# Head 0's queries in two halves, scores of one half beside the maxima of the other

## The chip, the cores and the metric

One NeuronCore of one Trainium2 chip runs the whole program. The metric is device time in microseconds (us), the median of several executions. Engines: TensorE multiplies (PE, its weight load PEld), VectorE (DVE), ScalarE (ACT) and GpSimd (POOL) compute, SyncE (SP) issues most DMAs.

## The reference, cut to what matters

Hashed-bucket attention (16 heads of 768 x 64), then two feed-forward layers over 1536 tokens. The change touches the attention alone.

```python
q_bits = (einsum(q, proj) > 0); k_bits = (einsum(k, proj) > 0)      # 6 bits
mask   = bucket(q_bits)[:, None] == bucket(k_bits)[None, :]
scores = where(mask, q @ k.T / sqrt(64), -1e9)
attn   = exp(scores - scores.max(-1)); attn = attn / (attn.sum(-1) + 1e-9)
x      = attn @ v                       # then x -> two feed-forward layers
```

## The kernel before, in words

Everything is float32; operands of TensorE are split into a rounded high part and a low part (`qB` and `qX` for queries, `KK[:, 0]` and `KK[:, 1]` for keys). Rows 0 to 13 of `qB` and `KK` hold the codes of the buckets as +-1 and large numbers, so that one product gives score and mask together; one more row carries minus the maximum of each query. A query's row maximum is taken from rounded operands first (`smax`, L392: two matmuls of 384 columns, then one reduction on VectorE over 2 x 385 PSUM columns, the last of each bank a fixed bound). The row of maxima goes into `qB`. Then `st` (L437) computes the transposed scores of 128 keys by 768 queries with four matmuls, and ScalarE takes Exp straight from PSUM into the tile `E[c]`. `pair` adds two such tiles on GpSimd, `pv` multiplies by the values, `dsum` sums the denominators.

Work is issued in slots, six for a head; slot 6h + c has `st(h, c)`, `smax(h + 1, c)` and whatever else is due. Each engine runs its own instructions in the order in which the program writes them. Before slot 0 comes a list written by hand, `start`, with its helpers: `get` and `load` (DMAs), `khi`, `qhi`, `klo`, `qlo` (head 0's splits), `codes` (code products), `code_k` on VectorE and `code_q` on ScalarE (signs into `KK` and `qB`), `warm(n)` (n products of ones, each shown as two entries, that do nothing but keep TensorE busy), `ident` (identity for the transpose), `row0` (head 0's maxima, turned from a column into a row by six matmuls with the identity; for the other heads `fin_a` on VectorE and the DMA `fin_b` do that), `move_k`, `move_x`, `move_h` (copies from one group of partitions to another by DMA). `hi` and `lo` split the heads behind. PSUM is eight banks, as four tiles `T` of two, given out in turn by `two_banks`.

Head 0 in `start`: its loads, products for codes, signs, six `smax`, head 1's codes, `row0`, then slot 0 begins with all 768 queries' scores.

Of the kernel before, what the change touches and what calls it, by code (L numbers as in the profile page):

```python
# [27 lines left out]
NBITS = 6  # L28
QUAD = S // 4
OLD = 3  # L30
EARLY = 7
W_AT, W_LEAD = 11, 6
POOL_LO = (("lo", 1), ("lo", 2))
# [14 lines left out]
def attention_moe_moe(ctx: ExitStack, tc: tile.TileContext, kq, v, proj2, cst, eye, w1, w2, ab, out):  # L48
# [11 lines left out]
    def f32(ap):  # L60
        return ap.bitcast(F32)
# [7 lines left out]
    def lo_pool(o, i, h):  # L69
        nc.gpsimd.tensor_tensor(out=o, in0=i, in1=f32(h), op=ALU.subtract)  # L70
# [88 lines left out]
    def attention(actx, tctx):  # L159
# [10 lines left out]
        ring[0] = pool(actx, "ring0", RING[0])  # L170
        ps = pool(actx, "ps", 1, space=PSUM)
        T = [ps.tile([128, 2, 512], F32, tag=f"s{i}", name=f"s{i}") for i in range(4)]
        turn = [0]
        ahead = []

        def two_banks():
            if ahead:
                return ahead.pop()
            turn[0] += 1
            return T[(turn[0] - 1) % 4]  # L180

# [19 lines left out]
        def memsets():  # L201
            nc.vector.memset(ones, 1.0)
            nc.vector.memset(wones, 1.0)
            for t in E:
                nc.gpsimd.memset(t[:, :, HALF:HALF + 2], GUARD / S)
            for t in T:
                nc.vector.memset(t[:, :, HALF:HALF + 1], -BIG / 4)
            nc.gpsimd.memset(f32(qB[0])[0:64], 0.0)
            pad(0, nc.gpsimd)
            pad(1, nc.vector)  # L210
            for i in range(2):
                nc.gpsimd.memset(f32(SM[i]), 0.0)
# [19 lines left out]
        def load(h):  # L232
            if not 0 <= h < B * H:
                return
            b, hh = divmod(h, H)
            if h == 0:
                home[0] = wpool.tile([128, 2, 2 * DM], F32, tag=f"w{EARLY - 1}", name="kq")
            raws[h] = home[0][:, h % 2, 0:S]
            nc.sync.dma_start(out=raws[h], in_=kq[b, hh])


        def load_v(j):
            if 0 <= j < B * H // 2:
# [13 lines left out]
                fn(qX[h % NB], raws[h], qB[h % NB])  # L257


        def khi(i):  # L260
            o = KK[0][64:128, i] if i < 2 else qX[0][0:64]
            nc.scalar.activation(out=o, in_=raws[0][0:64], func=ACT.Copy)

        def qhi():
            nc.vector.tensor_copy(qB[0][64:128], raws[0][64:128])

        def qlo():
            lo_pool(qX[0][64:128], raws[0][64:128], qB[0][64:128])

        def klo():  # L270
            lo_pool(qX[0][0:64], raws[0][0:64], qX[0][0:64])

        def move_k(h):
            if 0 <= h < B * H:
# [39 lines left out]
        def codes(h):  # L314
            if not 0 <= h < OLD:
                return
            p = [two_banks() for _ in range(1 + (h == 0))]
            ct[h] = p[0][:, 0], p[-1][:, 1]
            code_products(h)


        def warm(n):
            if not ahead:
                ahead.append(two_banks())
            for _ in range(n):
                nc.tensor.matmul(out=ahead[0][0:32, 0, 0:128], lhsT=ones, rhs=wones, start=True, stop=True)

        def code_k(h, of=(0, 1)):
            if not 0 <= h < OLD:
# [54 lines left out]
                )  # L384


        def signs(h):
            for a in range(2):
                code_k(h, (a,))
                code_q(h, (1 - a,))  # L390

        def smax(h, c):  # L392
            if not 0 <= h < B * H:
                return
            p = two_banks()
            m = SM[h % 2][:, c:c + 1] if h else Z[:, 32 + c:33 + c]
            for a in range(2):
                nc.tensor.matmul(  # L398
                    out=p[:, a, 0:HALF], lhsT=qB[h % NB][:, c * 128:(c + 1) * 128], rhs=qhalf(KK[h % NB][:, 0], a),
                    start=True, stop=True,  # L400
                )
            nc.vector.tensor_reduce(out=m, in_=p[:, :, 0:HALF + 1], op=ALU.max, axis=AX.XY)  # L402


        def fin_a(h):
# [10 lines left out]
                out=f32(qB[h % NB])[ROW:ROW + 1].rearrange("o (c i) -> o c i", c=NC), in_=ST[h % 2][0:NC],  # L416
            )

        def row0():
            p = two_banks()  # L420
            for c in range(NC):
                nc.tensor.matmul(
                    out=p[0:64, c // 3, c % 3 * 128:c % 3 * 128 + 128], lhsT=Z[:, c:c + 64], rhs=I_t,
                    start=True, stop=True,
                )
            nc.vector.tensor_copy(qhalf(qB[0], 1)[32:33], p[32:33, 1, 0:HALF])
            nc.scalar.activation(out=qhalf(qB[0], 0)[32:33], in_=p[32:33, 0, 0:HALF], func=ACT.Copy)

        def ident():
            hi_pool(I_t, I_f)  # L430
# [3 lines left out]

        pt = {}

        def st(h, c):  # L437
            if not 0 <= h < B * H:
# [12 lines left out]
            nc.scalar.activation(out=E[c][:, :, 0:HALF], in_=halves(p), func=ACT.Exp, scale=1.0 / D ** 0.5)  # L451
# [205 lines left out]
        def get(i):  # L657
# [2 lines left out]
            )[i]  # L660
            (nc.sync if i else nc.scalar).dma_start(out=t, in_=d)

        def coef():
# [12 lines left out]
        def run():  # L676
            memsets()
            fns = {o[0]: o[1] for o in order}
            fns.update(get=get, coef=coef, khi=khi, qhi=qhi, qlo=qlo, klo=klo, signs=signs, row0=row0, ident=ident, spare=spare)
            done.update((name, (0,)) for name in ("hi", "lo", "move_k", "code_ka", "code_kb", "code_q", "fin_b"))  # L680
            for name, *k in start:
                if name == "warm":
                    warm(*k)
# [237 lines left out]
        return run  # L921

    with tc.manual_schedule():
        nc.scalar.preload_act_table_set("natural_log_exp_and_others")
        tctx = ExitStack()
        with ExitStack() as actx:
            run, tail = attention(actx, tctx)
# [59 lines left out]
```

## Time and profile before

| what | value |
|---|---|
| median of 3 runs | 734.08 us (734.04 to 735.63) |
| the profiled execution | 734.39 us, of which its span 732.6 us |
| TensorE busy | 724.3 us, 99% of the span |
| VectorE, ScalarE, GpSimd busy | 575.9, 416.4, 130.3 us |
| DMA | 82.89 MB, mean 113 GB/s |

Times of rows count from the span's start. In a row, the name before the arrow is what is written, the one behind it what is read. `x8` is a count of merged instructions; a bracket gives the engine's idle time before the group and what ended it. Matmul ends are modelled, so a busy TensorE is not one at its peak; a float32 product of 128 columns counts as two entries.

### The profile page before, as it was taken

The page shows a single profiled execution, that of the slowest core. Times are in us where ns is not written, and L with a number is a line of the kernel's source. Part 1 is how long each engine was busy: PE and PEld are TensorE (multiplying, and loading weights), DVE is VectorE, ACT ScalarE, POOL GpSimd, SP SyncE. Part 2 cuts the span into 40 slices and gives each one's busy share as a digit, 9 for nine tenths or more (in the row PEclk, how much of TensorE's full clock was granted, in tenths as well). Part 3 has the DMA queues.
Part 4 walks back from the last instruction along what each step waited for, and adds up shares of the span by engine and source line. Part 5 has one row for each costly group of instructions (what it writes and reads, how often), then busy time and mean ns, then how long its engine had stood idle before and what let it go on. Part 6 is the DMA issues. An engine that isn't in the chain of part 4 may idle for free.

```text
span 732.6 us, 11610 instructions
## 1 busy us (share of the span) xinstructions
PE 724.3 (99%) x4212; PEld 577.1 (79%) x4212; DVE 575.9 (79%) x1042; ACT 416.4 (57%) x688; POOL 130.3 (18%) x108
## 2 busy tenths in 40 slices
PE   8999999999999999999999999999999999999997
PEld 6777777676778788888888888878888888888886
DVE  6878898988568994655556876599998888898886
ACT  5766767676644432212122334687877767777674
POOL 7657566665700000000000000000000000000000
PEclk9999999999999999999999999999999999999999
DMA  5777868885144442455446884200001000010001
GB/s 156 207 205 191 224 183 215 192 213 141 35 129 137 146 138 78 151 165 172 145 151 203 275 251 156 86 1 1 0 1 57 1 1 0 1 58 0 1 1 58
DMA packets 48505, 82.89 MB, mean 113 GB/s; under 512 B 6634, under 2 KB 24256, under 8 KB 48448
## 3 DMA queue, kind: packets, MB, share of 16 engines
q1 hardware_dynamic: 48123, 82.07, 38.6%
q8 instruction: 33, 0.54, 0.3%
q14 instruction: 25, 0.20, 0.1%
q10 hardware_dynamic: 324, 0.08, 0.1%
HBM read 55.71 MB, written 14.14 MB: 95 GB/s over the span
## 4 chain that ended last, share of the span: by engine, by line
PE 83%; DVE 7%; DMA 5%; issue 1%; ACT 1%; POOL 1%; SPq 0%; POOLq 0%; ACTq 0%; DVEq 0%
PE h L731 31%; PE y L751 17%; PE y L749 15%; PE s L446 7%; PE s L293 6%; PE s L398 4%; PE s L481 1%; DMA d<-rc 1%; DMA qB<-stt 1%; DVE w L73 1%; DVE t L106 1%; DVE r L109 1%; DVE z L402 1%; DVE gl L73 1%; DMA R<-d 1%
## 5 line engine op out<-in xcount | busy, mean ns | idle before, releaser
L731 PE MATMUL h<-xh,w 128*128 128x512 f32 x768 | 204.9, 389 | 0.0
L731 PEld LDWEIGHTS h<-xh,w 128*128 128x128 f32 x768 | 144.2, 188 | 30.3 <-issue 0.3
L73 DVE TENSOR_TENSOR gl<-ep,gh 128x512 fp32r<-128x512 f32 x96 | 66.0, 687 | 70.8 <-ACT ep L775 70.1
L774 ACT ACTIVATE gh<-h 128x512 fp32r<-128x512 f32 x48 | 28.7, 598 | 149.4 <-PE h L731 136.3
L731 PE MATMUL h<-xl,w 128*128 128x512 f32 x384 | 102.6, 389 | 0.0
L402 DVE TENSOR_REDUCE smt<-s 128x1 fp32r<-128x770 f32 x90 | 86.4, 960 | 19.5 <-PE s L398 14.4
L751 PE MATMUL y<-w,gh 128*128 128x512 f32 x384 | 96.3, 389 | 0.0
L749 PE MATMUL y<-gh,w 128*128 128x512 f32 x384 | 94.8, 389 | 0.0
L471 POOL TENSOR_TENSOR es<-e,e 128x768 f32<-128x768 f32 x48 | 89.3, 1863 | 16.4 <-ACT e L451 15.1
L451 ACT ACTIVATE e<-s 128x768 f32<-128x768 f32 x96 | 77.3, 814 | 19.2 <-PE s L446 15.6
L731 PEld LDWEIGHTS h<-xl,w 128*128 128x128 f32 x384 | 72.1, 188 | 15.0
L749 PEld LDWEIGHTS y<-gh,w 128*128 128x128 f32 x384 | 72.1, 188 | 14.9
L751 PEld LDWEIGHTS y<-w,gh 128*128 128x128 f32 x384 | 72.1, 188 | 14.9
L293 PE MATMUL s<-e,vf 128*32 128x386 f32 x768 | 65.2, 488 | 0.0
L781 ACT ACTIVATE ep<-h 128x512 f32<-128x512 f32 x48 | 28.5, 595 | 52.3 <-PE h L731 52.3
L109 DVE SCALAR_TENSOR_TENSOR r<-r,t 128x256 int32<-128x256 int32 (+1 forms) x114 | 52.1, 457 | 4.8
L106 DVE SCALAR_TENSOR_TENSOR t<-r,t 128x256 int32<-128x256 int32 (+1 forms) x114 | 52.3, 458 | 3.9
L783 DVE TENSOR_TENSOR n<-n,ep 128x512 f32<-128x512 f32 x48 | 33.1, 690 | 26.7 <-ACT n L782 26.7
L751 PE MATMUL y<-w,gl 128*128 128x512 f32 x192 | 53.3, 392 | 0.5 <-DVE gl L73 0.4
L749 PE MATMUL y<-gl,w 128*128 128x512 f32 x192 | 51.6, 390 | 0.4 <-DVE gl L73 0.4
L446 PE MATMUL s<-qB,kk 128*128 128x384 f32 x192 | 50.5, 343 | 1.0 <-DMA qB<-stt 0.7
L293 PEld LDWEIGHTS s<-e,vf 128*32 128x32 f32 x768 | 24.7, 110 | 32.7 <-issue 30.3
(84 smaller groups left out, 991.1 us busy)
## 6 DMA issues: line engine op xcount, KB each, us to landing
r<-w SPq DMA_DIRECT2D x100, 256.0 KB
w<-r SPq DMA_DIRECT2D x64, 128.0 KB
w<-w SPq DMA_DIRECT2D x16, 512.0 KB
r<-w SPq DMA_DIRECT2D x14, 512.0 KB
kq<-kq SPq DMA_DIRECT2D x16, 384.0 KB
kk<-qB SPq DMA_DIRECT2D x15, 384.0 KB
kk<-qX SPq DMA_DIRECT2D x16, 192.0 KB
qX<-qB SPq DMA_DIRECT2D x16, 192.0 KB
```

The lines of the kernel that those rows point to most:

```text
L73: nc.vector.tensor_tensor(out=o, in0=i, in1=f32(h), op=ALU.subtract)
L106: lambda: nc.vector.scalar_tensor_tensor(out=t, in0=r[:, :, 1], scalar=-0x40000000, in1=t, op0=ALU.bitwise_and, op1=ALU.bitwise_or),
L109: lambda: nc.vector.scalar_tensor_tensor(out=o, in0=r[:, :, 0], scalar=29, in1=t, op0=ALU.logical_shift_right, op1=ALU.bitwise_or),
L293: nc.tensor.matmul(out=o[32 * a:32 * a + 32, 0:HALF + 2], lhsT=w[:, a % 2 * 32:a % 2 * 32 + 32], rhs=x[:, a // 2], start=start, stop=stop,)
L402: nc.vector.tensor_reduce(out=m, in_=p[:, :, 0:HALF + 1], op=ALU.max, axis=AX.XY)
L446: nc.tensor.matmul(out=p[:, a, 0:HALF], lhsT=kk[:, c * 128:(c + 1) * 128], rhs=qq[:, a * HALF:(a + 1) * HALF], start=(i == 0), stop=(i == 1),)
L451: nc.scalar.activation(out=E[c][:, :, 0:HALF], in_=halves(p), func=ACT.Exp, scale=1.0 / D ** 0.5)
L471: nc.gpsimd.tensor_tensor(out=sums[h, c], in0=halves(pt[h, c]), in1=halves(pt[h, c + 1]), op=ALU.add)
L731: nc.tensor.matmul(out=p, lhsT=w[:, c * 128:(c + 1) * 128], rhs=x[:, c, :], start=(n == 0), stop=(n == 11))
L749: nc.tensor.matmul(out=y[m], lhsT=w[:, DM + m * 128:DM + (m + 1) * 128], rhs=g, **s)
L751: nc.tensor.matmul(out=y[m], lhsT=g[:, m * 128:(m + 1) * 128], rhs=w[:, DM:2 * DM], **s)
L783: nc.vector.tensor_tensor(out=v_, in0=v_, in1=u, op=ALU.mult)
```

## The change

Head 0's key and query load is split by columns into two DMAs (`load0`); the two DMAs that moved head 0's parts between partitions (`move_x(0)`, `move_h(0)`) give way to a computation at the target (`klo` writes `KK[0][0:64, 1]` directly, `qxhi` copies on ScalarE). Codes, signs and the row of maxima go by halves of 384 queries. `st0(c, a)` computes head 0's scores of 128 keys for half a; the six of half 0 are issued in `start`, between the maxima of half 1 and the row of half 1, and slots 0 to 5 hold those of half 1. Both copies of the row are ScalarE's. Head 0 and 1 have fixed PSUM banks. The maxima stand at columns 124 to 507 of a bank and their bound at 508, where neither sums nor scores write. The list has fewer `warm` products (4 + 3 + 1 + 1 in place of 5 + 4 + 1 + 1 + 1 + 5 + 6). Maxima of head 0 lie in every second column of `Z`. The table load of ScalarE is issued behind the first DMA.

```diff
+UP = 124
-        turn = [0]
-        ahead = []
+        turn = [3]
-                nc.vector.memset(t[:, :, HALF:HALF + 1], -BIG / 4)
+                nc.vector.memset(t[:, :, UP + HALF:UP + HALF + 1], -BIG / 4)
+        def load0(a):
+            if a == 0:
+                home[0] = wpool.tile([128, 2, 2 * DM], F32, tag=f"w{EARLY - 1}", name="kq")
+                raws[0] = home[0][:, 0, 0:S]
+            nc.sync.dma_start(out=qhalf(raws[0], a), in_=qhalf(kq[0, 0], a))
+        def khi0(a):
+            nc.scalar.activation(out=qhalf(KK[0][64:128, 0], a), in_=qhalf(raws[0][0:64], a), func=ACT.Copy)
...
-        def qhi():
-            nc.vector.tensor_copy(qB[0][64:128], raws[0][64:128])
+        def qhi(a):
+            nc.vector.tensor_copy(qhalf(qB[0][64:128], a), qhalf(raws[0][64:128], a))
+        def qxhi():
+            nc.scalar.activation(out=qX[0][0:64], in_=f32(qB[0][64:128]), func=ACT.Copy)
         def klo():
-            lo_pool(qX[0][0:64], raws[0][0:64], qX[0][0:64])
+            lo_pool(KK[0][0:64, 1], raws[0][0:64], qX[0][0:64])
...
-            p = [two_banks() for _ in range(1 + (h == 0))]
-            ct[h] = p[0][:, 0], p[-1][:, 1]
+            if h == 0:
+                ct[h] = T[0][:, 0], T[1][:, 1]
+            elif h == 1:
+                ct[h] = T[1][:, 0], T[1][:, 0]
...
-            p = two_banks()
-            m = SM[h % 2][:, c:c + 1] if h else Z[:, 32 + c:33 + c]
+            p = T[2 - h + c % 2] if h < 2 else two_banks()
+            m = SM[h % 2][:, c:c + 1] if h else Z[:, 32 + 2 * c:33 + 2 * c]
-                    out=p[:, a, 0:HALF], lhsT=qB[h % NB][:, c * 128:(c + 1) * 128], rhs=qhalf(KK[h % NB][:, 0], a),
+                    out=p[:, a, UP:UP + HALF], lhsT=qB[h % NB][:, c * 128:(c + 1) * 128], rhs=qhalf(KK[h % NB][:, 0], a),
-            nc.vector.tensor_reduce(out=m, in_=p[:, :, 0:HALF + 1], op=ALU.max, axis=AX.XY)
+            nc.vector.tensor_reduce(out=m, in_=p[:, :, UP:UP + HALF + 1], op=ALU.max, axis=AX.XY)
-        def row0():
-            p = two_banks()
-            for c in range(NC):
+        def row0(a):
+            p = T[1][:, 1]
+            for c in range(3 * a, 3 * a + 3):
                 nc.tensor.matmul(
-                    out=p[0:64, c // 3, c % 3 * 128:c % 3 * 128 + 128], lhsT=Z[:, c:c + 64], rhs=I_t,
+                    out=p[0:34, c % 3 * 128:c % 3 * 128 + 128], lhsT=Z[:, 2 * c:2 * c + 34], rhs=I_t,
-            nc.vector.tensor_copy(qhalf(qB[0], 1)[32:33], p[32:33, 1, 0:HALF])
-            nc.scalar.activation(out=qhalf(qB[0], 0)[32:33], in_=p[32:33, 0, 0:HALF], func=ACT.Copy)
+            nc.scalar.activation(out=qhalf(qB[0], a)[32:33], in_=p[32:33, 0:HALF], func=ACT.Copy)
+        def st0(c, a):
+            p = T[(0, 2 + a, 3 - 3 * a)[c // 2]][:, c % 2, 0:HALF]
+            for i in range(2):
+                nc.tensor.matmul(
+                    out=p, lhsT=KK[0][:, i, c * 128:(c + 1) * 128], rhs=qhalf((qB, qX)[i][0], a),
+                    start=(i == 0), stop=(i == 1),
+                )
+            pt[0, c] = E[c]
+            nc.scalar.activation(out=E[c][:, a, 0:HALF], in_=p, func=ACT.Exp, scale=1.0 / D ** 0.5)
...
         start = (
-            ("get", 0), ("load", 0), ("get", 1), ("load", 1), ("get", 3), ("get", 4), ("warm", 5), ("khi", 0), ("qhi",), ("codes", 0),
-            ("khi", 2), ("klo",), ("warm", 4), ("signs", 0), ("qlo",), ("ident",), ("hi", 1), ("khi", 1), ("get", 2), ("move_x", 0),
-            ("smax", 0, 0), ("move_k", 1), ("lo", 1), ("smax", 0, 1),
-            ("move_h", 0), ("load", 2), ("smax", 0, 2), ("warm", 1), ("move_x", 1), ("smax", 0, 3), ("warm", 1),
-            ("smax", 0, 4), ("warm", 1), ("smax", 0, 5), ("codes", 1), ("code_q", 1), ("fin_a", 0), ("warm", 5), ("row0",),
-            ("code_ka", 1), ("code_kb", 1), ("load_v", 0), ("move_h", 1), ("load", 3), ("spare",), ("hi", 2), ("lo", 2),
-            ("move_k", 2), ("warm", 6), ("st", 0, 0), ("coef",),
+            ("get", 0), ("table",), ("load0", 0), ("load0", 1), ("get", 1), ("load", 1), ("get", 3), ("get", 4), ("get", 2),
+            ("warm", 4), ("khi0", 0), ("qhi", 0), ("khi0", 1), ("qhi", 1), ("codes", 0), ("code_ka", 0), ("khi", 0),
+            ("code_kb", 0), ("code_qa", 0), ("klo",), ("ident",), ("qlo",), ("warm", 3), ("smax", 0, 0), ("code_qb", 0),
+            ("hi", 1), ("smax", 0, 1), ("move_k", 1), ("codes", 1), ("khi", 1), ("qxhi",), ("lo", 1), ("load", 2),
+            ("smax", 0, 2), ("warm", 1), ("code_qa", 1), ("load_v", 0), ("smax", 0, 3), ("move_x", 1), ("warm", 1),
+            ("smax", 0, 4), ("row0", 0), ("code_qb", 1), ("smax", 0, 5), ("move_h", 1), ("load", 3), ("spare",),
+            ("st0", 0, 0), ("st0", 1, 0), ("st0", 2, 0), ("st0", 3, 0), ("row0", 1), ("code_ka", 1), ("code_kb", 1),
+            ("st0", 4, 0), ("st0", 5, 0), ("hi", 2), ("lo", 2), ("move_k", 2), ("coef",),
         )
```

## Rows read from the trace of the kernel before

**Rows 1.** Waits of TensorE, whole span: us in total, times, longest

```profile
PE s L308 <- DMA pr<-proj: 0.8, 1, 0.8
PE s L446 <- DMA qB<-stt: 0.7, 2, 0.5
```

**Rows 2.** Windows: busy time (instructions) by engine, clock, DMA share, GB/s

```profile
80.00:120.00 40.00, 40.00 (x396) 29.47 (x398) 36.06 (x59) 27.35 (x43) 26.59 (x18) 1.00 0.78 198
```

**Rows 3.** Chain that ended last: start us, us, what

```profile
0.77 3.37 DMA pr<-proj
4.28 1.51 PE s L308 x8
5.78 1.66 PE s L326 x8
...
9.21 4.43 DVE z L402 x5
...
14.31 1.43 PE s L326 x12
...
36.57 3.41 DMA qB<-stt
...
147.91 2.88 DMA d<-rc
```

**Rows 4.** Timeline up to 16 us: start us, us, engine, what

```profile
3.99 0.84 ACT L262 ACTIVATE kk<-kq 64x768 fp32r<-64x768 f32 x1 [1.97 <-DMA kq<-kq]
...
5.77 1.80 POOL L70 TENSOR_TENSOR qX<-kq,qX 64x768 fp32r<-64x768 f32 x1 [1.12 <-ACT qX L262]
5.89 1.37 DVE L332 TENSOR_SCALAR kk<-s,cst 13x384 fp32r<-13x384 f32 x2 [1.34 <-PE s L308]
...
7.37 1.55 PE L398 MATMUL s<-kk,qB 128*128 128x384 f32 x6
...
8.33 5.29 DVE L402 TENSOR_REDUCE z<-s 128x1 fp32r<-128x770 f32 x6 [1.07 <-PE s L398]
...
11.51 0.85 PE L308 MATMUL s<-kq,pr 128*32 128x384 f32 x8
...
14.35 0.48 ACT L427 ACTIVATE qB<-s 1x384 fp32r<-1x384 f32 x1 [0.71 <-PE s L422]
...
14.93 1.37 DVE L332 TENSOR_SCALAR kk<-s,cst 13x384 fp32r<-13x384 f32 x2
```

**Rows 5.** Timeline of the loop of head 0 and up to head 1's scores

```profile
16.47 0.51 PE L398 MATMUL s<-kk,qB 128*128 128x384 f32 x2
...
16.67 0.82 ACT L451 ACTIVATE e<-s 128x768 f32<-128x768 f32 x1 [0.19 <-PE s L446]
...
17.02 6.16 DVE L402 TENSOR_REDUCE smt<-s 128x1 fp32r<-128x770 f32 x6 [0.71 <-PE s L398]
...
22.11 0.85 PE L308 MATMUL s<-kq,pr 128*32 128x384 f32 x8
...
22.57 0.84 ACT L64 ACTIVATE qB<-kq 128x768 fp32r<-128x768 f32 x1
22.76 1.84 POOL L471 TENSOR_TENSOR es<-e,e 128x768 f32<-128x768 f32 x1 [0.24 <-ACT e L451]
22.78 0.51 PE L353 MATMUL s<-kq,p 128*32 128x192 f32 x8
...
24.14 1.28 ACTq L415 DMA_DIRECT2D qB<-stt  x1
...
27.45 1.17 ACT L499 ACTIVATE ev<-s,vb 64x384 f32<-64x384 f32 x2
...
28.08 0.62 PE L446 MATMUL s<-qB,kk 128*128 128x384 f32 x2
```

**Rows 6.** Timeline of SP, issues of head 2's and head 3's loads

```profile
10.90 0.47 SPq L239 DMA_DIRECT2D kq<-kq  x1
...
16.95 1.30 SPq L239 DMA_DIRECT2D kq<-kq  x1
```

More of the change, by code (lines that the diff above doesn't have):

```diff
@@ L172, in attention @@
         T = [ps.tile([128, 2, 512], F32, tag=f"s{i}", name=f"s{i}") for i in range(4)]
-        turn = [0]
-        ahead = []
+        turn = [3]
         def two_banks():
-            if ahead:
-                return ahead.pop()
             turn[0] += 1
@@ L235, in load @@
             b, hh = divmod(h, H)
-            if h == 0:
-                home[0] = wpool.tile([128, 2, 2 * DM], F32, tag=f"w{EARLY - 1}", name="kq")
             raws[h] = home[0][:, h % 2, 0:S]
             nc.sync.dma_start(out=raws[h], in_=kq[b, hh])
+        def load0(a):
[3 more added lines that the diff above has]
+            nc.sync.dma_start(out=qhalf(raws[0], a), in_=qhalf(kq[0, 0], a))
         def load_v(j):
@@ L257, in lo @@
                 fn(qX[h % NB], raws[h], qB[h % NB])
+        def khi0(a):
+            nc.scalar.activation(out=qhalf(KK[0][64:128, 0], a), in_=qhalf(raws[0][0:64], a), func=ACT.Copy)
         def khi(i):
-            o = KK[0][64:128, i] if i < 2 else qX[0][0:64]
+            o = KK[0][64:128, 1] if i else qX[0][0:64]
             nc.scalar.activation(out=o, in_=raws[0][0:64], func=ACT.Copy)
-        def qhi():
-            nc.vector.tensor_copy(qB[0][64:128], raws[0][64:128])
+        def qhi(a):
+            nc.vector.tensor_copy(qhalf(qB[0][64:128], a), qhalf(raws[0][64:128], a))
+        def qxhi():
+            nc.scalar.activation(out=qX[0][0:64], in_=f32(qB[0][64:128]), func=ACT.Copy)
         def qlo():
@@ L316, in codes @@
                 return
-            p = [two_banks() for _ in range(1 + (h == 0))]
-            ct[h] = p[0][:, 0], p[-1][:, 1]
+            if h == 0:
+                ct[h] = T[0][:, 0], T[1][:, 1]
+            elif h == 1:
+                ct[h] = T[1][:, 0], T[1][:, 0]
+            else:
+                p = two_banks()
+                ct[h] = p[:, 0], p[:, 1]
             code_products(h)
         def warm(n):
-            if not ahead:
-                ahead.append(two_banks())
             for _ in range(n):
-                nc.tensor.matmul(out=ahead[0][0:32, 0, 0:128], lhsT=ones, rhs=wones, start=True, stop=True)
+                nc.tensor.matmul(out=T[0][0:32, 1, 0:128], lhsT=ones, rhs=wones, start=True, stop=True)
         def code_k(h, of=(0, 1)):
@@ L384, in quad_in @@
                 )
[L387 to L390, printed above, removed]
         def smax(h, c):
@@ L435, in attention @@
         pt = {}
+        def st0(c, a):
[7 more added lines that the diff above has]
+            nc.scalar.activation(out=E[c][:, a, 0:HALF], in_=p, func=ACT.Exp, scale=1.0 / D ** 0.5)
         def st(h, c):
+            if h == 0:
+                st0(c, 1)
+                return
             if not 0 <= h < B * H:
@@ L661, in get, with table @@
             (nc.sync if i else nc.scalar).dma_start(out=t, in_=d)
+        def table():
+            nc.scalar.preload_act_table_set("natural_log_exp_and_others")
         def coef():
@@ L678, in run @@
             fns = {o[0]: o[1] for o in order}
-            fns.update(get=get, coef=coef, khi=khi, qhi=qhi, qlo=qlo, klo=klo, signs=signs, row0=row0, ident=ident, spare=spare)
-            done.update((name, (0,)) for name in ("hi", "lo", "move_k", "code_ka", "code_kb", "code_q", "fin_b"))
+            fns.update(
+                get=get, coef=coef, khi=khi, khi0=khi0, qhi=qhi, qxhi=qxhi, qlo=qlo, klo=klo, row0=row0, ident=ident,
+                spare=spare, st0=st0, load0=load0, table=table, code_qa=lambda h: code_q(h, (0,)),
+                code_qb=lambda h: code_q(h, (1,)),
+            )
+            done.update((name, (0,)) for name in ("load", "hi", "lo", "move_k", "move_x", "move_h", "fin_b"))
+            done.update(("code_q", (h,)) for h in (0, 1))
             for name, *k in start:
@@ L923, in attention_moe_moe @@
     with tc.manual_schedule():
-        nc.scalar.preload_act_table_set("natural_log_exp_and_others")
         tctx = ExitStack()
```

## The prediction

> **What bounds the kernel now.** I read the waits of TensorE over the whole trace first. Behind the first code products, which wait 0.8 us for the projection, it waits 0.7 us in two pieces for a row of maxima, and for little else [rows 1]. Then the windows: TensorE is busy 40.00 of 40 us in a stretch of the attention heads [rows 2]. So nothing behind head 0 can be won without less TensorE work, and the change takes none away there. But what starts earlier ends earlier: time saved in the first 28 us should reach the end nearly whole. The chain of waits says what those 28 us consist of: projection load, code products, warm-up products, six maxima on VectorE, twelve warm-up entries, and only then scores [rows 3]. The timeline gives each engine's piece. VectorE ends head 0's maxima at 8.33 + 5.29 = 13.62 (M below), copies half of the row, writes head 1's codes from 14.93 to 16.30, and starts head 1's maxima at 17.02 = M + 3.40 [rows 4, 5]. They end at 23.18 (R), and head 1's scores start at 28.08 = R + 4.90 (F) [rows 5].
>
> **Part 1: the loads.** Head 0's keys and queries come in two halves. Before, one load of 384 KB is issued at 0.75 and ScalarE starts on it at 3.99 [rows 4]; a half should be there some 0.5 sooner. That alone moves nothing, as the products wait for the projection: issued 0.77, 3.37 us, products at 4.28 [rows 3]. Its queue sits beside the key load. Bounds for its new duration: 3.41, the row load of only 3 KB (nothing gained), and 2.88, the quickest row of the chain [rows 3]. At the start little else is in the queues, so I take the latter: products at 0.77 + 2.88 + 0.14 = 3.79, gain 0.49, ends 0 and 0.65. The second half and the small constants are issued one issue (0.45) later than now; no row waits for the constants, and codes on VectorE start only after the first products (at 4.7), which covers them.
>
> The same 3.4 us for 32 KB and for 3 KB [rows 3] can mean own latency or a neighbour's packets. The Trainium skill, "DMA: Bandwidth & Descriptors", section "Queues, rings and completion order", says that a DMA engine goes round its queue rows packet by packet. By it a projection packet waits for one key packet each time, and half-long key packets let it through sooner, as I take it. If only latency counts, this term is 0 and the sum is -2.0.
>
> **Part 2: up to the first maxima.** Before, eight warm-up entries of 1.92 stand between codes and maxima; after, six, and the other early ones lie in the shade of the load. 2 x 0.21 = -0.43 (1.66 for eight entries [rows 3]). TensorE reaches the first maxima at 7.37 - 0.49 - 0.43 = 6.45. Is all else ready? First products end some 0.85 after 3.79; two code halves of 0.69 each on VectorE end by 6.1; ScalarE has two key halves of 0.5, a whole of 0.84 [rows 4] and one Sign of 0.6 (nearest row: 1.17 for two of 64x384 with a bias [rows 5]) from 3.45 on, also by 6.1. So warm-ups stay the last to end. Against this stands the clock: the windows print a granted clock of 1.00, but eight code products take 1.51 at 4.28 and 0.85 at 11.51 [rows 3, 4], the lower level (1.2 GHz) and the upper (2.4). The rise lies inside the six maxima products of 1.55 at 7.37; if it stays at that instant, the pair that now starts at 6.45 runs wholly at the lower level and costs 0.15 more. VectorE starts at 7.57 instead of 8.33: -0.76. Six maxima at the old pace (head 1's code products, 0.85, fit between the second and the third) give M = 12.86.
>
> **Part 3: from M to head 1's maxima.** Removed: VectorE's half of the row copy and its wait for the row (M to 14.93, 1.31), twelve warm-up entries, the full scores ahead of the first maximum. VectorE may write head 1's codes at once, M + 0.03 to M + 1.40. Now the limit is ScalarE, whose queue is in program order. The first half-row's copy (0.48 [rows 4]) needs the third maximum only and ends by M - 1.4; a Sign (0.6) follows to M - 0.8; then four Exp of 384 columns. No row has such an Exp: 128x768 takes 0.82, 64x384 with a bias 0.59 [rows 5], 1x384 0.48 [rows 4]; I take 0.5, at a pitch of 0.4, ends 0.4 and 0.82. They end at M + 0.9; the second half-row's copy ends at M + 1.35, so the first second-half score product starts at M + 1.45 to M + 1.65, the maxima product 0.35 behind it (a loop step's six products take 1.04, part 4), VectorE 17.02 - 16.47 = 0.55 later [rows 5]: M + 2.56. Against M + 3.40: -0.84. Ends: -1.29 (VectorE's codes last: M + 1.40 + 0.71) and +0.5 (Exp at 0.82). The local copies that replace two DMAs (0.84 each on ScalarE, 1.80 each on POOL [rows 4]) end by 9.2, ahead of the first score at M - 1.4.
>
> **Part 4: the loop of head 0.** Before, one step is four score products and two for a maximum, and six maxima take 6.16 on VectorE [rows 5], against 5.29 at the start [rows 4]: TensorE sets the pace, 1.04 a step. After, half of the scores lie in part 3's shade; a step is 0.35 + 0.35 = 0.70 of TensorE, VectorE needs 0.87. Gain 6.16 - 5.29 = -0.87; ends -0.87 and 0, as maxima alternate between two bank pairs instead of four (refilling takes 0.55, which fits into 0.87). Parts 2 to 4: -0.76 - 0.84 - 0.87 = -2.47, R = 20.7.
>
> **Part 5: behind R.** F = R + 4.90: four transposes, the DMA issue (1.28, [rows 5]), and the row's landing. TensorE's own work from head 2's codes to F is 28.08 - 22.11 = 5.97, less the end of a wait [rows 1, 5]. It now starts about R - 1.4 instead of R - 1.07, so it ends by R + 4.4 and the row stays last. The last pair sum on POOL ends at 24.60 = M + 11.0 [rows 5]; its chain hangs on ScalarE's conversion of head 2 at M + 2.6, and ends near M + 11 again, while the denominators start at M + 11.5: 0.5 us of slack is left of 2. Head 3's codes need its load, issued at 16.95 for 1.30 and in use by 22.57 [rows 5, 6]. It goes out behind a move that waits for an earlier move's landing; as many bytes stand ahead as now, but head 2's load, now held until 10.90 [rows 6], leaves at 9.3 with POOL's last copy, so I expect it all about 1.2 sooner, just enough for TensorE at 19.7. From F on, all repeats as before. The bounds' new column, the maxima's offset of 124 and the changed order of banks have the same counts of elements: nothing.
>
> **Sum.** 734.39 (profiled: span 732.6 and 1.8 around it) - 2.47 = 731.9. That execution lies 0.31 above the median of 734.08, so 731.6. A measurement of this kernel tells about 0.3% (2.2 us) from no change: faster means below 731.9.
>
> **Rivals.**
> A. The clock rises later, since fewer warm-up entries run. For it: at the lower level code products (1.51) delay the third maximum by some 0.8, and each maxima step with its warm-up takes 0.70 + 0.43 = 1.13 instead of 0.87. Against: TensorE still has no gap from 3.8 to the maxima. Part 2 is lost: -0.84 - 0.87 = -1.7, 732.4. The rows show one execution only. The Trainium skill, "TensorE: Matmul & The Clock Gate", Part 1, says that the rise is not tied to the program's start and moves from run to run; no run here shows it move. Chance 0.14.
> B. Head 3's load comes no sooner. It lands at 22.57 at the latest and TensorE stands at head 3's codes until then, with 28.08 - 22.78 = 5.3 behind it [rows 5]: F = 27.9 at worst; with its earliest landing (16.95 + 3.2 = 20.2) nothing is lost. Middle: 21.4, F = 26.7, -1.4, 732.7. For it: move and load chain through landings. Chance 0.14.
> C. The halves do not overlap as meant: ScalarE, with twelve Exp in place of six and the second row copy behind four of them, holds the scores back. Exp at 0.82 gives +0.5 in part 3, and part 4 keeps its 0.87 only partly: -0.76 + 0.5 - 0.4 = -0.7, 733.4. Against: 0.48 for 384 columns. Chance 0.08.
> D. Slower: between M and head 1's maxima TensorE waits for the second row copy and its clock falls to the lower level. Then a loop step costs 1.4 instead of 0.87, 6 x 0.53 = 3.2 later, and the products behind it (5.97 at the upper level) lose another 1: 734.1 - 2.5 + 4.2 = 735.8. It decides once a step at the lower level exceeds VectorE's 0.87, which it does. For it: the twelve warm-up entries at 14.31 [rows 3], which kept TensorE busy there, are gone. Against: seven score and row pieces fill M - 1.4 to M + 1.1. Chance 0.06.
>
> **How the numbers follow.** Forecast (all parts, give or take 0.5): 0.58. Its own range is 731.0 to 732.2, on the faster side three times in four. The low end 730.9 adds the best of parts 1 and 3 in part; the high end takes in A, B and most of C: 733.3. Faster: 0.58 x 0.75 plus a little of A and B = 0.48. Slower by over 0.3% only in D: 0.06. Within: 0.46.
>
> **What would show it.** First code products at about 3.8, first maxima near 6.5, VectorE's maxima of head 0 from 7.6 to 12.9, of head 1 from 15.4 in 5.3 us, first scores of head 1 near 25.6, wait for the row there no more than 0.7. Wrong if products still start at 4.28 (part 1), if six maxima of head 1 take 6.1 (part 4), if head 3's code products wait for a load (B), or if matmuls of head 0 take twice their time (A, D); and all of it if the heads behind give the lead back.

## The result and the profile after

The changed kernel takes 741.41 us (median of 4, 740.68 to 743.97) against 734.37 for the kernel before in the same session: 1.0096 times as long, 95% interval 1.0081 to 1.0111. Forecast were 731.6 and a range of 730.9 to 733.3: wrong in sign, by 10 us. The profiled execution of after took 743.97 us (span 742.2), 2.6 above its median; what follows measures its span against 732.6 before, so it accounts for 9.6 us, where the medians differ by 7.0.

The waits of TensorE up to 31 us (us in total, times, longest). Of those in [rows 1] only the first, for the projection, falls into this stretch before:

```profile
PE s L445 <- ACT e L450: 2.5, 5, 0.6
PE s L337 <- ACT qB L352: 1.3, 1, 1.3
...
PE s L428 <- ACT qB L352: 1.1, 1, 1.1
PE s L316 <- DMA pr<-proj: 0.5, 1, 0.5
```

TensorE's timeline (start, length, operation, idle before it and what ended it):

```profile
3.60 1.70 PE L316 MATMUL s<-kq,pr 128*32 128x384 f32 x8 [0.51 <-DMA pr<-proj]
6.54 0.84 PE L337 MATMUL s<-wones,ones 128*32 128x128 f32 x6 [1.25 <-ACT qB L352]
7.32 0.97 PE L404 MATMUL s<-kk,qB 128*128 128x384 f32 x4
...
12.54 0.37 PE L428 MATMUL s<-eye,z 128*34 128x128 f32 x3 [1.10 <-ACT qB L352]
...
33.86 0.62 PE L464 MATMUL s<-qB,kk 128*128 128x384 f32 x2
```

VectorE's, and two lines of ScalarE's:

```profile
5.22 1.37 DVE L343 TENSOR_SCALAR kk<-s,cst 13x384 fp32r<-13x384 f32 x2 [0.60 <-issue]
8.04 4.43 DVE L408 TENSOR_REDUCE z<-s 128x1 fp32r<-128x770 f32 x5 [1.45 <-PE s L404]
13.35 0.96 DVE L408 TENSOR_REDUCE z<-s 128x1 fp32r<-128x770 f32 x1 [0.88 <-PE s L404]
18.57 1.35 DVE L343 TENSOR_SCALAR kk<-s,cst 13x384 fp32r<-13x384 f32 x2 [4.27 <-ACT qB L432]
21.48 0.96 DVE L408 TENSOR_REDUCE smt<-s 128x1 fp32r<-128x770 f32 x1 [1.55 <-PE s L404]
...
26.11 2.85 DVE L408 TENSOR_REDUCE smt<-s 128x1 fp32r<-128x770 f32 x3 [0.23 <-PE s L404]
```

```profile
5.92 1.28 ACT L352 ACTIVATE qB<-s,cst 14x384 fp32r<-14x384 f32 x2 [0.67 <-DVE kk L343]
...
11.92 0.57 ACT L352 ACTIVATE qB<-s,cst 14x384 fp32r<-14x384 f32 x1 [2.25 <-POOL kk L218]
```

The windows (busy time and count by engine, then granted clock, DMA share, GB/s):

```profile
12.00:16.00 4.00, 2.61 (x11) 1.47 (x11) 1.43 (x2) 2.58 (x6) 1.46 (x6) 0.90 0.54 198
16.00:20.00 4.00, 2.92 (x10) 2.27 (x11) 1.34 (x2) 1.91 (x4) 0.00 (x0) 0.50 0.51 147
...
24.00:28.00 4.00, 3.77 (x19) 2.75 (x22) 3.38 (x5) 1.83 (x4) 3.08 (x2) 0.82 0.69 176
```

The products start 0.7 us sooner than before, at 3.60. Then TensorE waits seven times (L337 and L428 for signs, L445 five times) for an engine that delivers it no operand. Head 0's last maximum ends at 14.31 (before 13.62 [rows 4], forecast 12.86), head 1's first starts at 21.48 (17.02 [rows 5], forecast 15.4), the last ends at 28.96 (23.18, forecast 20.7), and head 1's scores start at 33.86 instead of 28.08: 5.78 us later. From 16 to 20 us the granted clock is 0.5, the lower level, to which it fell at 15.21, in a stretch in which TensorE was busy 2.61 of 4 us.

Behind head 0 three more waits are new or longer, here those from 31 us to the end:

```profile
PE y L776 <- DVE gl L74: 2.6, 2, 2.1
PE s L464 <- DMA qB<-stt: 1.7, 2, 1.4
PE s L464 <- ACT dv L528: 1.0, 1, 1.0
```

Set against the trace of before by the starts of the same products, the delay is 5.78 at head 0's first value product, 6.86 at the first product of the feed-forward layers (the 1.0 for `dv` and 1.4 for a row of maxima are in it, less what was regained in other places), 9.06 at their seventh block (a block is twelve products) and 9.12 at their last. So 5.8 us are lost at head 0, 1.1 in the heads behind, and 2.2 at the start of the layers; the other 0.46 of the 9.58 lie behind the last product. The piece at the layers' start shows on SP's queue and on VectorE:

```profile
229.88 0.34 SPq L549 DMA_DIRECT2D d<-rc  x1
233.07 1.26 SPq L557 DMA_DIRECT2D R<-d  x2
234.44 7.55 SPq L867 DMA_DIRECT2D r<-w  x6
```

```profile
239.14 0.29 DVE L104 TENSOR_SCALAR t<-r 128x256 int32<-128x256 int32 x1 [3.55 <-DMA r<-w]
```

The same views of the kernel before:

```profile
223.02 0.34 SPq L531 DMA_DIRECT2D d<-rc  x1
224.39 1.26 SPq L539 DMA_DIRECT2D R<-d  x2
225.75 18.60 SPq L840 DMA_DIRECT2D r<-w  x11
```

```profile
230.06 0.29 DVE L103 TENSOR_SCALAR t<-r 128x256 int32<-128x256 int32 x1 [1.33 <-DMA r<-w]
```

`R<-d` reads what `d<-rc` writes, so it is issued once that 6 KB write has landed: 1.37 us behind its issue before, 3.19 after. The weight loads `r<-w` stand behind it in the queue, and VectorE, which converts the weights for TensorE, waits 3.55 us for one of them.

### The profile page after: what moved, and what is told of

Read it like the earlier page. It is cut to its first block, busy times and chain, and to the rows that moved or that the text cites. A ratio compares the mean times of both kernels' runs of the same rounds, so it can differ in the third digit from the quotient of the medians.

```text
span 742.2 us, 11551 instructions
## 1 busy us (share of the span) xinstructions
PE 725.5 (98%) x4184; PEld 575.8 (78%) x4184; DVE 576.1 (78%) x1042; ACT 418.9 (56%) x697; POOL 129.7 (17%) x108
## 4 chain that ended last, share of the span: by engine, by line
PE 87%; DVE 6%; DMA 3%; ACT 2%; issue 1%; SPq 0%; ACTq 0%; DVEq 0%
PE h L758 31%; PE y L778 17%; PE y L776 15%; PE s L464 8%; PE s L301 8%; PE s L404 4%; PE s L499 2%; PE s L445 1%; DMA r<-w 1%; DVE w L74 1%; DVE t L107 1%; PE s L364 1%; DVE gl L74 1%; DVE r L110 1%; DMA kk<-qB 1%
## 5 line engine op out<-in xcount | busy, mean ns | idle before, releaser
L469 ACT ACTIVATE e<-s 128x768 f32<-128x768 f32 x90 | 72.7, 815 | 19.4 <-PE s L464 16.1
L404 PE MATMUL s<-kk,qB 128*128 128x384 f32 x192 | 50.3, 344 | 0.0
```

The source lines that it names most:

```text
L404: nc.tensor.matmul(out=p[:, a, UP:UP + HALF], lhsT=qB[h % NB][:, c * 128:(c + 1) * 128], rhs=qhalf(KK[h % NB][:, 0], a), start=True, stop= ...
```

## The experiments

The theory for head 0: these waits are made for a whole tile `T` of two PSUM banks. Where two engines use one tile, the second waits for the first, also when they touch different banks, and also when both only read. The warm-up products (bank 1 of T0) then wait for ScalarE's reading of codes in bank 0; the first row product (T1) for head 1's codes, which ScalarE's queue brings to their turn only at 11.92; each second half score (two products) for the Exp of the half score before it, which lies in the other bank of its tile; and VectorE's codes of head 1 (T1) for ScalarE's copy of the second row, 4.27 us. The rival is the clock, or ScalarE's twelve Exp. The first four runs undo one piece each, the fifth all of them.

**The last head's tile.** After starts its turn of tiles at 3 instead of 0; a loop that lines up the last head then skips three tiles at once and lands on the tile that the denominators still hold. The edit skips them singly, in heads 5, 8 and 11:

```diff
+            if c == 3 and h in (5, 8, 11):
+                turn[0] += 1
             p = two_banks()
```

> Changed kernel with one thing undone: the turn of the PSUM tiles is moved on by one in heads 5, 8 and 11, so that it need not jump by three tiles ahead of the last head. In the changed kernel's trace the last head's first score product waits 0.96 us for the denominators' eviction of the head before, as the jump gives it the tile just used. Theory W (waits made by shared PSUM tiles): this wait goes and the time falls by 1.0, to about 739.8 to 740.4. Theory C (all of it is the clock that falls in the start): no change, 740.7 to 741.4.

740.64 us, 1.0076 (1.0055 to 1.0097). The wait for `dv` is gone: the delay against before, which jumps by 1.01 us between heads 14 and 15 in after, does not move there. Of that jump 0.62 comes back in after by the layers' first product, so the edit is worth 0.4, not the 1.0 expected. By luck this run also prices the clock: up to 28 us it is the same program as after, but the granted clock rose later (10.22 instead of 4.97) and then stayed at the upper level,

```profile
16.00:20.00 4.00, 2.44 (x13) 1.75 (x13) 1.33 (x2) 2.55 (x7) 0.00 (x0) 1.00 0.55 147
```

and its head 0 ends 3.75 us later than before, not 5.78. The two clocks differ by 2.0 of the 5.8, and that is a net price: the late rise has its own cost, as head 0's maxima end at 14.89 here and at 14.31 in after. So 3.75 are lost without the fall, the late rise among them. In the timed executions of after, too, the slowdown does not hang on the fall: 742.06 us at a mean clock of 1.000, 740.77 at 0.999. The layers of this run start without a loss too (`R<-d` follows 1.37 behind `d<-rc`).

**Scores in different tiles.**

```diff
-            p = T[(0, 2 + a, 3 - 3 * a)[c // 2]][:, c % 2, 0:HALF]
+            p = T[((2, 3, 2, 3, 2, 3), (0, 3, 0, 3, 3, 0))[a][c]][:, c // 2 % 2, 0:HALF]
```

> Changed kernel with other PSUM tiles for head 0's half scores: neighbours in order of issue never lie in one two-bank tile. Theory W: the five waits of 0.58 for the Exp before (2.5 us in all) go, head 1's scores start 1.5 to 2.5 sooner, 739 to 740. Theory C: the waits are only where the clock's loss shows; 741 give or take 0.7. Theory M (ScalarE's queue stands behind head 1's signs, which wait for a DMA): less than 0.5 gained, as the queue ahead is the same.

741.23 us, 1.0086 (1.0058 to 1.0113). The waits of 2.5 us for Exp shrink to one line, and head 1's maxima run nearly closed up:

```profile
PE s L445 <- ACT e L450: 0.2, 1, 0.2
```

```profile
17.48 1.35 DVE L343 TENSOR_SCALAR kk<-s,cst 13x384 fp32r<-13x384 f32 x2 [2.94 <-ACT qB L432]
19.54 5.40 DVE L408 TENSOR_REDUCE smt<-s 128x1 fp32r<-128x770 f32 x6 [0.71 <-PE s L404]
```

Head 0 ends only 1.60 us later than before; against the run above, where the clock was much the same (risen at 9.56 here), that is 2.15 us less. VectorE's wait behind the row copy stays (2.94). But the total did not move, where 739 to 740 were expected: 2.4 us are lost in the heads behind, the last head's jump among them, and 2.6 at the layers' start, where `R<-d` came 3.43 us behind `d<-rc`.

**The row in another tile.**

```diff
-            p = T[1][:, 1]
+            p = T[0][:, 1]
```

> Changed kernel with the row of maxima in tile 0 in place of tile 1, which holds head 1's code products. Theory W: TensorE no longer stands 1.1 us at the row's first half until head 1's signs have been read, and head 0's last maximum ends near 12.9 in place of 14.3; VectorE writes head 1's codes at about 14 in place of 18.6. But the score products behind it still go one by one with their Exp, so head 1's maxima start only 0.5 to 1.5 sooner: 739.9 to 740.9. Theory C: no change. Theory M: no change before the signs (11.9), since the copy of the row stays behind them on ScalarE.

742.04 us, 1.0093 (1.0066 to 1.012). The wait of the row product is gone and VectorE's codes no longer wait for the copy:

```profile
7.81 5.29 DVE L408 TENSOR_REDUCE z<-s 128x1 fp32r<-128x770 f32 x6 [1.45 <-PE s L404]
13.37 1.35 DVE L343 TENSOR_SCALAR kk<-s,cst 13x384 fp32r<-13x384 f32 x2 [0.26 <-ACT qB L352]
19.68 0.96 DVE L408 TENSOR_REDUCE smt<-s 128x1 fp32r<-128x770 f32 x1 [4.96 <-PE s L404]
```

Head 0's maxima end at 13.10 instead of 14.31. Then the paired scores (3.0 us of waits) hold head 1's first maximum, and the idle time only moves from one line of VectorE to another. The time expected, 739.9 to 740.9, was missed; the clock fell here too, at 18.29, and head 0 ends 4.66 later than before.

**The warm-up products in another tile.**

```diff
-                nc.tensor.matmul(out=T[0][0:32, 1, 0:128], ...
+                nc.tensor.matmul(out=T[t][0:32, 1, 0:128], ...      # t = 3 for the three ahead of the maxima
```

> The changed kernel with the three warming products between codes and first maxima writing tile T3 in place of the free bank of tile T0. Theory (waits are made for whole tiles): the wait of 1.25 us of TensorE for the first code copy goes, but the first product of the maxima still waits for that copy's data, so the first maximum and the end move by under 0.4 us: 740 to 742. Rival (the wait is for the operand qB, not for the tile): the warming products still start at 6.54.

The first theory holds on the wait: the warm-up products start at 4.82, behind the codes' products, and not at 6.54.

```profile
4.82 1.49 PE L337 MATMUL s<-wones,ones 128*32 128x128 f32 x6
6.56 1.33 PE L404 MATMUL s<-kk,qB 128*128 128x384 f32 x4 [0.26 <-ACT qB L352]
```

It missed on the time: 743.86 us, 1.0133 (1.0108 to 1.0157), above the 1.0096 of after, though the two intervals just touch. The maxima start 0.76 sooner on TensorE, yet M is 14.20 against 14.31, since the row product waits 1.4 in place of 1.1 for codes that ScalarE does at 11.81 (11.92 in after). In the profile the clock is at the lower level from 14.23 up to 28 us (0.51 in the window of 24 to 28, where after had 0.82), and head 0 ends 6.77 later than before. An earlier start only made the gap behind it longer.

**All four, and an order of the list to suit them.** Both signs of head 1 are done behind the first row copy, and one maximum of head 1 is taken between the scores:

```diff
-            ("smax", 0, 4), ("row0", 0), ("code_qb", 1), ...
-            ("st0", 0, 0), ("st0", 1, 0), ("st0", 2, 0), ("st0", 3, 0), ("row0", 1), ("code_ka", 1), ("code_kb", 1),
+            ("smax", 0, 4), ("row0", 0), ("code_qa", 1), ("code_qb", 1), ...
+            ("st0", 0, 0), ("st0", 1, 0), ("row0", 1), ("code_ka", 1), ("code_kb", 1), ("st0", 2, 0), ("smax", 1, 0),
+            ("st0", 3, 0),
```

> Changed kernel with all of these waits taken away together: warm-ups ahead of the maxima in a tile of their own, the row in tile 0, head 1's signs behind the first row copy, half scores in alternate tiles, the second row half and head 1's first maximum moved ahead of the last half scores, and the turn moved on in single steps. Theory W: head 0's maxima end near 12.8, head 1's maxima run from about 15 to 20.7, its scores start near 25.6, and the time is what was predicted for the change, 731.5 to 733. Theory C: with the clock falling as before some 3 us stay lost, 735 to 738. Theory M alone: about 737.

737.8 us, 1.0045 (1.0032 to 1.0059): 3.6 us better than after, still slower than before. Head 0 now ends where it did before (-0.08).

```profile
7.45 5.29 DVE L408 TENSOR_REDUCE z<-s 128x1 fp32r<-128x770 f32 x6 [0.77 <-PE s L404]
...
15.24 0.96 DVE L408 TENSOR_REDUCE smt<-s 128x1 fp32r<-128x770 f32 x1 [0.71 <-PE s L404]
18.40 0.96 DVE L408 TENSOR_REDUCE smt<-s 128x1 fp32r<-128x770 f32 x1 [2.20 <-PE s L404]
19.53 3.73 DVE L408 TENSOR_REDUCE smt<-s 128x1 fp32r<-128x770 f32 x4 [0.17 <-PE s L404]
```

M is 12.74 and head 1's first maximum 15.24, as forecast (12.86, 15.4). The second comes at 18.40, behind five half scores. TensorE waits four times (0.9 in all) for Exp, and ScalarE, with twelve Exp of some 0.49, the second row copy and a conversion of 0.84 between them, waits six times for TensorE between its first Exp and its last (2.3 us from 13.16 to 22.27): the two take turns. The last maximum ends at 23.26, where before had 23.18. So theory W holds for the start (12.8 and 15) and fails on the rest (20.7 and 731.5 to 733); the time lies in the range of theory C, but in the profile the clock rose at 6.79 and did not fall.

**Without the halves of the scores.** Row, warm-ups and signs as above, but scores in whole rows of 768 queries as in the kernel before: `p = two_banks() if h else T[2 + c % 2]`, `st0` unused, both row copies in the list ahead of the first scores, head 1's maxima in T0 and T1, and a turn of tiles that starts at 2 and needs no jump.

> Changed kernel without the halves of the scores (whole scores of 768 queries in the loop, two tiles of their own, head 1's maxima in the other two), with the row in tile 0, head 1's signs behind the first row copy and the warm-ups in a tile of their own. Theory A (twelve Exp of 384 columns in place of six of 768 make ScalarE, and the one-tile waits between them, the bound of head 0's loop): head 1's maxima start near 15.2 and run at TensorE's pace, 1.04, to about 21.5; head 1's scores start near 26.4, 1.6 sooner than before, and the time is 732.5 to 735, better than the arrangement with halves (737.8). Rival: the halves as such win: then this one ends no earlier than the arrangement with halves.

735.72 us, 1.0015 (1.0002 to 1.0028), better than with the halves, as expected, though not under 735. Head 0 ends 0.76 earlier than before (1.6 were expected), although the clock was at the lower level from 14.74 to 18.15. So a good part of what can be won at head 0 needs no halves at all (with them, in their best order below, it is 1.18). At the last product it is 1.21 later than before: `R<-d` comes 2.63 behind `d<-rc`, VectorE waits 2.52 for a weight load.

**The bound's column alone,** in the kernel before (`UP = 124`, as in the change).

> Kernel before with one part of the change alone: the maxima at columns 124 to 507 of a bank and the bound at 508. Theory: the same counts of elements, so the same time as before, 734 to 736. Rival (the offset costs later: both experiments whose head 1 starts with the kernel before still end 2 to 3 us later): 736.5 to 738.

735.3 us, 1.0007 (0.9997 to 1.0016): no difference, as forecast.

**The halves in their best order.** As all four, with head 1's maxima in T0 and T1 and spread among the second half's scores, the half scores in T2 and T3 by turns, a turn that starts at 2, and head 2's conversion behind the seventh Exp. In this run head 2's low part is taken behind its signs, so rows 0 to 13 of that low part are not the reference's.

```diff
-            p = T[2 - h + c % 2] if h < 2 else two_banks()
+            p = T[2 - 2 * h + c % 2] if h < 2 else two_banks()
+            ("st0", 3, 0), ("st0", 4, 0), ("smax", 1, 1), ("st0", 5, 0), ("st", 0, 0), ("hi", 2), ("move_k", 2), ("coef",),
+            ("smax", 1, 2), ("st", 0, 1), ("st", 0, 2), ("smax", 1, 3),
```

> Changed kernel with the halves kept and all that stood in their way moved: maxima of head 1 in two tiles of their own and ahead of the second-half scores on TensorE, half scores in the other two, head 2's conversion behind the seventh Exp, head 2's remainder on GpSimd behind the pair sums, and a turn of tiles that needs no jump. Theory A: ScalarE still has 8.7 us of work from 11 us on, with gaps between Exp in alternate tiles; head 1's maxima run from 15.2 to about 21, scores of head 1 start near 25.8, 2.2 sooner than before: 732.5 to 735. Rival (halves lose whatever the order): maxima end at 22 or later, 736 to 738.

736.69 us, 1.0028 (1.0014 to 1.0043): on the time and on the end of the maxima (22.06) the rival's marks came true, not the theory's. Even so head 0 ends 1.18 sooner than before, the lead is still 1.20 at the layers' first product, and 0 at the seventh block. SP and VectorE there:

```profile
221.82 0.34 SPq L549 DMA_DIRECT2D d<-rc  x1
224.88 1.27 SPq L557 DMA_DIRECT2D R<-d  x2
226.26 5.71 SPq L871 DMA_DIRECT2D r<-w  x4
```

```profile
230.07 0.29 DVE L104 TENSOR_SCALAR t<-r 128x256 int32<-128x256 int32 x1 [2.55 <-DMA r<-w]
```

`d<-rc` is issued 1.20 sooner than before and lands 0.49 later.

**The jump of the last head alone,** in the kernel before: `turn = [1]` for `turn = [0]`.

> Kernel before with one number changed: the turn of the PSUM tiles starts at 1 in place of 0, so that it has to jump by three tiles ahead of the last head, as in the changed kernel, and the last head's scores fall on the tile of the denominators just computed. Theory W: 0.9 to 1.0 us slower than before, 735 to 737, with a wait of 0.96 on ScalarE's eviction at that place. Rival (the wait only takes time that would be lost there anyway): no change.

735.4 us, 1.0004 (0.9995 to 1.0014). The wait is there:

```profile
194.10 0.61 PE L446 MATMUL s<-qB,kk 128*128 128x384 f32 x2 [0.96 <-ACT dv L510]
```

and the time is the same, as the rival has it. The offset from before goes from -0.66 at head 14 to +0.36 at head 15, and is back at -0.26 by the layers' first product: TensorE no longer waits 0.4 us for the last sum of Exp, as it does in before. At the layers' seventh block it is -0.01. So a lead, whether 0.26 here or 1.20 in the run above, is gone by the layers' seventh block. That points to SP's queue, which the last runs test.

**Weight loads ahead of the spreading.** The three loads of the layers' fourth step are issued ahead of the two `R<-d`, so that they no longer wait for the landing of `d<-rc`:

```diff
-            for g in {2: range(last, last + 5), 3: range(last + 5, last + 7), ...
+            for g in {2: range(last, last + 5), 3: (last + 5,), 3.5: (last + 6,), ...
...
                     for fn, k in now:
                         if fn in group:
                             fn(*k)
+                if i == 3:
+                    tail(3.5)
```

In the halves' best order (with head 2's low part whole again), in the kernel before, and without halves. The expectations call the feed-forward layers the mixture:

> The halves in their best order (e9), with head 2's low part taken one step earlier, ahead of its signs, and the three weight loads of the mixture's fourth step put on SP's queue ahead of the spreading of the last sums. Theory (the lead of head 0 is lost at the mixture's start because SP holds the weight load behind the spreading): the load is issued near 224.6 instead of 226.26, VectorE's wait for it falls from 2.55 to under 1.4, TensorE's two waits for gl (1.6) go, and a lead of about 1.0 us at the first product of the mixture reaches the end: 0.7 to 1.2 us under the kernel before, ratio 0.9984 to 0.9990. Rival (the mixture sets its own pace from another resource): the end stays within 0.3 us of before whatever SP's order is.

> The kernel before with the same exchange on SP's queue alone. Both theories: no change (734.4 to 735.4), since there the load at 225.75 follows VectorE's release of its buffer at 225.75 at once and the spreading was through by 225.65. If it is faster by over 1 us, SP's queue was a bound of its own.

> Whole scores (e7) with the exchange on SP's queue. Theory: the lead of 0.8 us at head 0 is kept as far as the heads keep it (in e7's profile it had gone by the mixture's first product, +0.01), so 0.0 to 0.8 us under before at the end, against +1.2 in e7. Rival (other pace): as e7, 1.0 to 1.5 us over before.

734.1 us, 0.9989 (0.9981 to 0.9998); 734.05 us, 0.9985 (0.9976 to 0.9994); and 732.76 us, 0.9974 (0.9963 to 0.9986), the fastest of all and below both kernels. SP's queue in the first:

```profile
226.69 1.28 SPq L870 DMA_DIRECT2D r<-w  x3
228.06 1.27 SPq L557 DMA_DIRECT2D R<-d  x2
```

VectorE's wait for a weight load is at most 0.3 us in all three. What was lost between the layers' first product and their last turns into a gain over the trace of before: 1.54 to 0.62 in the first, 1.28 to 0.38 in the second, -0.68 to -1.61 in the third. The rival, a pace of the layers' own, falls. Three expectations missed. Without halves the gain is larger than the 0.0 to 0.8 expected. In the kernel before I had expected nothing: its load at 225.75 was held by SP too, some 0.6 us (in all three runs it leaves 0.6 sooner against TensorE's products), and its wait of 1.33 cost about 0.9. And the lead of the halves' best order got lost this time between heads 1 and 7, -1.24 to +0.94; TensorE waits there 1.7 us for rows of maxima (`qB<-stt`) and 1.6 for weight conversions on VectorE. Waits of this kind move from execution to execution of all these kernels (before 0.7 us for the rows, 2.3 in the second run here). The last section has what goes with the longest of those for rows; the cause of the others stays open. Whether whole scores with the earlier loads beat the exchange alone is not settled either: 0.9963 to 0.9986 against 0.9976 to 0.9994.

## Why the prediction was wrong

**Part 1 held.** Products at 3.60 (forecast 3.79), the projection in 2.81 us. Whether that is latency or shorter packets beside it no run separates.

**Part 2 failed, and first of all,** at the sentence "So warm-ups stay the last to end". I took the two banks of a tile for independent. First, the code products run 1.70 us and do not end after 0.85, so VectorE's codes begin at 5.22. Then ScalarE's signs, which read other partitions of the same bank of T0 (32 to 45, VectorE 0 to 12), wait for VectorE's reading (5.92), and the warm-up products, in T0's other bank, wait 1.25 for the signs. In the kernel before the two engines took the two halves of the codes, which lie in two tiles, in opposite order and so read side by side (VectorE from 5.89 [rows 4]):

```profile
5.92 1.24 ACT L341 ACTIVATE qB<-s,cst 14x384 fp32r<-14x384 f32 x2 [0.23 <-issue]
```

With the warm-up products in T3 the maxima start at 6.56 (forecast 6.45), and wait 0.26 for a sign: there too the warm-ups are not the last to end. (2 x 0.21 is 0.42, not 0.43; nothing hangs on it.) The gain of 0.76 was 0.29 in after, and 0.88 in the run with all four edits.

**Part 3 failed** at "VectorE may write head 1's codes at once": they stood behind ScalarE's second row copy, through tile T1, and that behind score pairs that took turns with their Exp. The first maximum of head 1 came 7.2 us behind M, not 2.56; with all four edits and the new order, which takes that maximum ahead of the last three half scores, 2.50. The term was wrong on what waits for what. I also missed that ScalarE's first sign of head 1, at 11.92, waits for a move that reads the rows it overwrites; the three row products stood behind it. Its row names POOL, which was long done; the chain of waits has the move there, landing at 11.81:

```profile
7.96 3.85 DMA kk<-qB
```

**Part 4 failed together with part 3.** In after the loop took 7.5 us instead of 5.29, at the lower clock and with paired tiles. With the scores' tiles apart it took 5.40, so the count of a step was right. But there head 1's first maximum comes 5.0 behind M, and where it comes 2.5 behind M the loop takes 8.0 from the first maximum to the last (all four) or 6.8 (best order). The two parts were added as if each could be had without the other: from M to R the forecast has 7.85, before took 9.56, and these three runs, with the clock at the upper level, took 10.4, 10.5 and 9.4. That is nearest to rival C, to which I gave 0.08. Its main argument, that 0.48 us for an Exp is short, overlooked that ScalarE's other work does not go away: 7.64 of the 11 us from 13 to 24 in the run with all four, here above the same stretch of the kernel before:

```profile
13.00:24.00 11.00, 9.70 (x66) 6.57 (x69) 7.57 (x12) 7.64 (x17) 6.49 (x8) 1.00 0.67 182
13.00:24.00 11.00, 10.67 (x86) 8.95 (x88) 9.01 (x14) 7.67 (x12) 7.72 (x10) 1.00 0.79 215
```

ScalarE is no busier than before, and TensorE is less busy: with twelve short Exp in place of six long ones the two wait for each other. That ScalarE alone bounds the loop is not shown, since it stands idle 2.3 us for scores.

**Part 5 failed** at two sentences. That "the changed order of banks" costs "nothing": in after it cost a wait of 1.0 us at the last head, of which 0.4 stayed. "From F on, all repeats as before", and with it the opening claim that time saved should reach the end nearly whole: a lead of up to 1.2 us ended at the layers' start, where SP held the weight loads behind the landing of a 6 KB write (shown by the last three runs). I had read the waits of TensorE alone, where this place shows with a single wait of 0.4; the wait of 1.33 on VectorE ahead of it was in the trace.

**The rivals.** A did not occur in after, where the clock rose at 4.97, sooner than before. A later rise did come in the first experiment, the same program up to there (10.22); whether fewer warm-up entries had to do with it is not shown. D came nearest, and with too small a chance (0.06): TensorE did stand idle and its clock did fall, but that is a net 2.0 us of 5.8, and the idle time came from tiles. B did not occur: head 3's codes waited for no load.

On the waits, the Trainium skill, "PSUM — Partial Sum Buffer", section "PSUM bank collisions raise a hardware error", says that the compiler's scheduler puts any two engines that touch one bank on the same 32 partitions in sequence, reads included. The traces agree on reads, and in this program the unit is larger, a tile of two banks: ScalarE's signs wait for VectorE's read of other partitions (5.92), VectorE's codes of head 1 wait 4.27 us for ScalarE's read of the other bank (gone once the row is in T0), and the 1.25 us at 6.54 are gone once the warm-up products write T3.

## What to carry to other kernels

Before engines are to work side by side on PSUM, list for every step which tile each one touches, reads too, and give each pair that shall overlap a tile of its own, or let the two take their pieces in opposite order. Where a piece is split to overlap, count both engines' whole queues over that stretch, and add two gains only if one order of instructions gives both. And before a gain at the start is booked at the end, look along the in-order DMA queue for an issue that waits for a landing with loads behind it.

## What had not been expected of the hardware

The landing of the same 6 KB write, read as the time from the issue of `d<-rc` to that of `R<-d`, took 1.37 us in four profiled executions (before, the last head's tile, the column alone, the jump alone), 1.38 in a fifth, and 2.6 to 3.5 in six others. SP's issues ahead of it are nearly the same in all; the DMA packets of the traces differ. From the issue of `d<-rc` to that of `R<-d`, after has one packet on a further queue, which the profile calls that of instructions (queue, kind, packets, MB, share):

```profile
q8 instruction: 1, 0.02, 2.0%
q1 hardware_dynamic: 64, 0.01, 1.4%
```

The kernel before has none there:

```profile
q1 hardware_dynamic: 64, 0.01, 3.2%
```

In all eleven executions at least 45 of the write's 48 packets end within 1.01 us. In the six slow ones the last three end at 1.55 to 2.44, each time 0.03 to 0.05 behind the end of that 16 KB packet (2.06 behind 2.03 in after). In the five quick ones there is no such packet (three), or it begins at 1.20 and 1.24, when the write's packets are done. All ten traces of after and its variants have the packet, 0.54 to 1.42 us behind the issue, and in eight of them the write's last packets end behind it; none of the four of the kernel before and its variants has it. So it is the changed program that meets it, and not in every execution. Why its instructions are loaded just there no run tests, and not all of the delay is explained: in after the last packet ends 1.06 us later than in before, and the landing comes 1.8 later. The same packets go with the four longest waits for rows of maxima, 1.40 to 1.45 us (after, the column alone, and the first two runs with earlier loads): there one of the row's six packets ends at 3.51 to 3.55 us behind its issue instead of about 2.65, 0.05 to 0.06 behind a 16 KB instruction packet.

The rise of TensorE's clock lies at 7.90 us in the trace of before and at 4.97 in that of after; over all kernels here it lies between 4.5 and 10.2, although TensorE's first products start within 0.3 us of each other in all that share the new loads. After and the first experiment, the same program up to 28 us, had it at 4.97 and 10.22, and only the one that rose early fell back. The Trainium skill, "TensorE: Matmul & The Clock Gate", Part 1, says that the rise moves from run to run, in its example by half a microsecond; the traces agree that it moves, but here by 5.2 us between the two executions just named.
